# Moving the second layer's six matmuls in between the two parts of the attention result

## The chip, the cores and the metric

The kernel runs on one core of one Trainium2 chip. The time is the device time of one execution in microseconds. The median of four runs is compared; the profile is of one execution.

## The reference

Two stages follow each other, in float32. The first is a linear attention with a decaying state (batch 4, heads 8, sequence 768, head dimension 48):

```python
for t in range(S):
    cur = np.einsum('bhd,bhe->bhde', u[None] * kt, vt)
    y[:, :, t] = np.einsum('bhd,bhde->bhe', rt, state + cur)
    state = wt[:, :, :, None] * state + np.einsum('bhd,bhe->bhde', kt, vt)
```

Its output, turned to x of (B·S, H·D) = 3072 x 384, goes through a feed-forward layer with d_ff = 2048:

```python
h = x @ w_in
g = h - np.tanh(h)
return (g @ w_out).astype(np.float32)
```

## The kernel before, in words

**Blocks.** The 4 x 768 tokens are cut into eight blocks of 384 tokens (`NB`). The attention of a block is computed in chunks of 64 tokens (`L`), six to a block, for four pairs of heads; two heads of a pair lie on partitions 0 to 47 and 64 to 111. The attention of block 0 is computed ahead of everything by `boot`. Then the main loop (lines 626 to 666) runs over i = 0 to 7: it computes the feed-forward layer of block i (`here`, its input tile `xT`) and, in between, the attention of block i + 1 (`later`). So there are seven blocks in the loop that hold attention work; the last has none. "Block 0" below is the loop's turn i = 0.

**The feed-forward layer.** d_ff is cut into 16 chunks f of 128. For each f, `first` issues the first layer for 384 tokens: three float32 matmuls of 128x128 by 384, which the profile shows as six MATMULs into `hp` (line 471). It also issues six ScalarE operations, beginning with the copy of `hp` into `h` (line 478). The elementwise rest is five VectorE operations, issued in the next turn of f. `Second.add` issues the second layer: three float32 matmuls into three accumulators `acc` in PSUM, again six MATMULs in the profile (line 509). It runs three chunks late: at f the main loop adds chunk f − 3 (`LAG`), so at f = 13 it adds chunk 10. `hp` has one buffer in PSUM, `acc` three of one each, and the attention's `att` two.

**The attention's phases.** `plan` gives each f at most one phase of the next block's attention: level 1 and the levels 2 to 32 (the scores inside a chunk, by doublings), "turn" (transposes of the keys), "update" (the states at the six chunk borders, with VectorE operations at line 371), and "result" at f = 13. Each phase is issued between the first layer of its f and the second layer. The matmuls of a phase use 48- or 64-row pieces of the array.

**The result phase.** `result` adds up two products in two PSUM tiles `yp` (both buffers of `att`). Part one is 96 matmuls of the states with the decayed receptance `rp` (line 391). Then a drain of TensorE raises the semaphore `fence` (line 397) and TensorE waits for it (line 399). Part two is 96 matmuls of the values with the scores `A` onto the same sums (line 409). Four ScalarE copies take the result from PSUM into `late` and the three parts of the next block's `xT` (line 423). Then `fill_holes` issues six small DMAs on SP (line 431), which put the heads that lie in `late` into the 16-partition holes of `xT`. The next block's first layer at f = 0 reads `xT` with its holes.

**What sets the order.** The instructions of TensorE, SP, VectorE and ScalarE are issued in the order in which the code stands (`manual_schedule`). In one turn of f the order is: the first layer; the elementwise rest of f − 1; what `before` holds; the phase; what `behind` holds; the load of this f, if there is one (on SP, bound by `begin_behind` to start after the copy of `hp` of this f); the conversions of weights, in the turn i = 0 alone; the second layer of f − 3. At f = 13, `plan` has a load (of `wt`) only for i = 0; at f = 14 there is one of `kq` for i = 0 and of `rp` for the other turns.

Of the kernel before, what the change touches and what calls it, by code (L numbers as in the profile page):

```python
# [54 lines left out]
NPAIR = H // 2  # L55
# [29 lines left out]
def kernel(  # L85
# [79 lines left out]
    def convert(f, raw, _):  # L165

        lo, hi = raw[:, :, 0], raw[:, :, 1]
        a = w_sb[:, f, :].bitcast(I32)
        up = conv.tile([P, 2 * DM], I32, name="up", tag="up", bufs=3)
        nc.scalar.activation(out=a.bitcast(F32), in_=hi.bitcast(F32), func=AF.Prelu,  # L170
                             scale=HIGH_SCALE, alpha=NEGATIVE)
        nc.scalar.activation(out=up, in_=lo.bitcast(U32), func=AF.Copy, scale=2.0 ** -29)
        return [
            lambda: nc.vector.tensor_single_scalar(a, a, 3, op=ALU.logical_shift_left),
            lambda: nc.vector.tensor_tensor(out=a, in0=a, in1=up, op=ALU.add)]  # L175


    def scratch(ps):
        return ps.tile([P, 2, BANK], F32, name="att", tag="att")
# [3 lines left out]
    class Block:  # L183
# [189 lines left out]
                        in1=kvp[:, c % 2, n0:n0 + D], op0=ALU.mult, op1=ALU.add)  # L373
            return ins

        def result(self, ps, pairs, holes_full=False):


            St, rp = states[self.q], self.tiles["rp"]
            yp = [scratch(ps) for e in range(2)]  # L380
            slots = [pairs[n:n + 2] for n in range(0, len(pairs), 2)]
            for n, slot in enumerate(slots):
                for c in range(NCP):
                    for par in range(2):
                        for p in slot:
                            for h in range(2):
                                rows = slice(64 * h, 64 * h + D)
                                e0 = 64 * (h ^ (p % 2))
                                t0 = p * NB + (2 * c + par) * L
                                n0 = (n * NCP + c) * L  # L390
                                nc.tensor.matmul(yp[p % 2][e0:e0 + 64, par, n0:n0 + L],  # L391
                                                 lhsT=St[rows, p, 2 * c + par, :],
                                                 rhs=rp[rows, t0:t0 + L],
                                                 start=(n == 0 and c == 0), stop=False,
                                                 skip_group_check=True)

            nc.tensor.drain().then_inc(fence, 1)
            fences.append(None)
            nc.tensor.wait_ge(fence, len(fences))
            for n, slot in enumerate(slots):  # L400
                for p in slot:
                    for c in range(NCP):
                        for h in range(2):
                            for par in range(2):
                                toks = slice(64 * par, 64 * par + 64)
                                e0 = 64 * (h ^ (p % 2))
                                f0 = p * D2 + h * D
                                n0 = (n * NCP + c) * L
                                nc.tensor.matmul(yp[p % 2][e0:e0 + D, par, n0:n0 + L],  # L409
                                                 lhsT=self.v[toks, c, f0:f0 + D],  # L410
                                                 rhs=A[toks, h, p, c, :],
                                                 start=False,
                                                 stop=(n == len(slots) - 1 and c == NCP - 1),
                                                 skip_group_check=True)
            copies = []
            for n, slot in reversed(list(enumerate(slots))):
                for p in reversed(slot):
                    src = yp[p % 2][:, :, n * NCP * L:(n + 1) * NCP * L].rearrange(
                        "e a (c t) -> e c a t", t=L)
                    dst = self.xT[:, p, :] if p < KC else self.late  # L420
                    dst = dst.rearrange("e (c a t) -> e c a t", a=2, t=L)
                    for rows in (slice(0, D), slice(64, 64 + D)) if holes_full else (slice(0, P),):
                        copies.append(nc.scalar.copy(out=dst[rows], in_=src[rows]))  # L423
            return copies[0]

        def fill_holes(self, engines):

            for n in range(2 * KC):
# [2 lines left out]
                engines[n % len(engines)].dma_start(out=self.xT[64 * h + D:64 * h + 64, i, :],  # L431
                                                    in_=self.late[src:src + 16, :])


        def phase(self, ps, name):
            if name == "level 1":
                for p0 in HALVES:
                    self.level_1(ps, p0)()
            elif name == "turn":
                for p0 in HALVES:  # L440
                    self.turn(ps, p0)
            elif name == "update":
                for p0 in HALVES:
                    self.update(ps, p0)
            elif name == "result":
                self.result(ps, list(range(NPAIR)))
                self.fill_holes([nc.sync])
            else:
                self.level(ps, name, 0, NPAIR)
# [67 lines left out]

    def plan(i):

        names = ("level 1", 2, 4, 8, 16, 32, "turn", "update", "result")  # L520
        if i == 0:

            steps = (1, 2, 3, 4, 6, 8, 10, 11, 13)
            before, behind = {0: ("totals 1", "kq", "rp")}, {1: ("totals 2",)}
            converted = (1, 3, 3, 4, 5, 7, 10, 10, 12, 13)
            loads = {f: "weights" for f in (1, 2, 3, 4, 6, 7, 8, 9, 10)}
            loads.update({5: "v", 11: "rmix", 12: "kmix", 13: "wt", 14: "kq", 15: "rp"})
        else:
            steps = (4, 5, 6, 7, 8, 9, 10, 11, 13)
            before = {0: ("kmix",), 1: ("rmix",), 2: ("totals 1",), 3: ("totals 2", "kq"), 4: ("rp",)}  # L530
            behind, converted = {}, ()
            loads = {2: "v", 5: "rmix", 7: "kmix", 9: "wt", 11: "kq", 14: "rp"}
        return dict(zip(steps, names)), before, behind, converted, loads
# [5 lines left out]
    def more_weights(queue):  # L539
        raws.append(load_weights(more_weights.n, queue))  # L540
        more_weights.n += 1
        return raws[-1][-1]
# [3 lines left out]
    def begin_behind(ins, dma):  # L546


        tc.add_manual_dep(dma.ins, ins.ins.name, mybir.DependencyInfo(
            mybir.DependencyClass.Sync, mybir.DependencyReason.DATA))  # L550
# [73 lines left out]
    ps_a = ctx.enter_context(tc.tile_pool(name="ps_a", bufs=2, space=PSUM))  # L624
    waiting, rest, extra = [], [], []
    for i, blk in enumerate(blocks):
        here = xT
        later = blocks[i + 1] if i + 1 < len(blocks) else None
        after = blocks[i + 2] if i + 2 < len(blocks) else None
        if later:  # L630
            xT = later.begin()
        phases, before, behind, converted, loads = plan(i)
        second = Second(blk.b * S + blk.q * NB, ps_d)
        for f in range(NF):
            g, next_rest, made = first(here, f, ps_d)
            waiting.append((second, f, g))

            for n, op in enumerate(rest):
                op()
                if n >= 2 and extra:  # L640
                    extra.pop(0)()
            for op in extra:
                op()
            rest = next_rest
            if later:
                for name in before.get(f, ()):
                    later.prepare(name)
                if f in phases:
                    later.phase(ps_a, phases[f])
                for name in behind.get(f, ()):  # L650
                    later.prepare(name)
            name, ins = loads.get(f), None
            if name == "weights":
                ins = more_weights(nc.sync)
            elif name == "v":
                ins = later.load_v() if later else None
            elif name and after:
                ins = after.load(name, {"r": rT, "k": kT, "w": wT}[name[0]], 0, NPAIR)
            if ins:
                begin_behind(made, ins)  # L660
            extra = []
            for _ in range(converted.count(f)):
                extra += convert(*raws.pop(0))
            if len(waiting) > LAG:
                s, fs, gs = waiting.pop(0)
                s.add(fs, gs)
    for op in rest:
        op()
    for s, fs, gs in waiting:
# [48 lines left out]
```

## Time and profile before

| | |
|---|---|
| median of 4 runs | 673.24 us (671.71 to 674.21) |
| profiled execution | 674.21 us, its span 672.5 us |
| mean granted TensorE clock | 0.982 |
| TensorE matmul (PE) busy | 644.9 us, 96% |
| TensorE weight loads (PEld) busy | 414.2 us, 62% |
| VectorE (DVE) busy | 545.4 us, 81% |
| ScalarE (ACT) busy | 489.0 us, 73% |
| HBM traffic | 47.19 MB read, 4.72 MB written |

PE is the matmuls, PEld the weight loads; one sequencer issues both, and a load can run beside a matmul. SPq is a DMA queue's issue on SyncE. In the timelines of the profile each line is a run of like instructions: start and length in microseconds from the start of the span, engine, line of the kernel, operation, out<-in by the program's names, tile shape and count. What stands in brackets is the engine's idle time ahead of it, and what ended it: "issue" where the profile shows nothing that it waited for, "PEq" for TensorE's own sequencer. The length of a run of matmuls goes to the end of its last one, which overlaps the next run, so steps between runs are read from start to start.

### The profile page before, as it was taken

The page shows a single profiled execution, that of the slowest core. Times are in us where ns is not written, and L with a number is a line of the kernel's source. Part 1 is how long each engine was busy: PE and PEld are TensorE (multiplying, and loading weights), DVE is VectorE, ACT ScalarE, POOL GpSimd, SP SyncE. Part 2 cuts the span into 40 slices and gives each one's busy share as a digit, 9 for nine tenths or more (in the row PEclk, how much of TensorE's full clock was granted, in tenths as well). Part 3 has the DMA queues.
Part 4 walks back from the last instruction along what each step waited for, and adds up shares of the span by engine and source line. Part 5 has one row for each costly group of instructions (what it writes and reads, how often), then busy time and mean ns, then how long its engine had stood idle before and what let it go on. Part 6 is the DMA issues. An engine that isn't in the chain of part 4 may idle for free.

```text
span 672.5 us, 19961 instructions
## 1 busy us (share of the span) xinstructions
PE 644.9 (96%) x8480; PEld 414.2 (62%) x8480; DVE 545.4 (81%) x1101; ACT 489.0 (73%) x966; POOL 4.6 (1%) x19
## 2 busy tenths in 40 slices
PE   5867999999999999999999999999999999999998
PEld 4745656566665666656665666656666566655554
DVE  7769998799877997589975998769986899746664
ACT  4668699885867767785776858677577867768785
POOL 2000000000000000000000000000000000000000
PEclk9958899999999999999999999999999999999999
DMA  8645254422111313121312222113131200000000
GB/s 318 226 166 186 84 173 158 147 75 90 56 51 54 117 52 96 56 72 49 96 49 57 72 80 66 50 55 109 60 95 38 91 2 3 2 11 35 1 0 35
DMA packets 30840, 54.36 MB, mean 81 GB/s; under 512 B 2336, under 2 KB 28704, under 8 KB 30752
## 3 DMA queue, kind: packets, MB, share of 16 engines
q1 hardware_dynamic: 30336, 52.80, 24.2%
q8 instruction: 66, 1.08, 0.7%
q10 hardware_dynamic: 352, 0.25, 0.1%
q14 instruction: 22, 0.18, 0.1%
q0 software_dynamic: 64, 0.05, 0.0%
HBM read 47.19 MB, written 4.72 MB: 77 GB/s over the span
## 4 chain that ended last, share of the span: by engine, by line
PE 74%; DVE 9%; ACT 5%; issue 5%; PEld 4%; DMA 1%; PEldq 1%; SPq 0%; DVEq 0%
PE acc L509 32%; PE hp L471 29%; PE att L242 8%; DVE states L371 2%; PE att L409 2%; PEld att L391 2%; PEld hp L471 2%; PE att L342 2%; DVE w_sb L175 1%; PEld acc L509 1%; DVE rp L274 1%; PE att L319 1%; DVE hs L488 1%; DVE scores L302 1%; ACT qb L481 1%
## 5 line engine op out<-in xcount | busy, mean ns | idle before, releaser
L471 PE MATMUL hp<-xT,w_sb 128*128 128x384 f32 x768 | 273.1, 492 | 3.2 <-ACT xT L423 2.1
L509 PE MATMUL acc<-w_sb,gT 128*128 128x384 f32 x768 | 275.8, 496 | 0.0
L471 PEld LDWEIGHTS hp<-xT,w_sb 128*128 128x128 f32 x768 | 147.7, 193 | 107.1 <-issue 3.6
L509 PEld LDWEIGHTS acc<-w_sb,gT 128*128 128x128 f32 x768 | 141.3, 191 | 89.5 <-ACT o L514 2.3
L478 ACT ACTIVATE h<-hp 128x384 f32<-128x384 f32 x128 | 62.8, 491 | 143.9 <-PE hp L471 143.2
L493 DVE TENSOR_TENSOR th<-h,th 128x384 f32<-128x384 f32 x128 | 70.9, 554 | 47.3 <-ACT th L482 47.2
L488 DVE SCALAR_TENSOR_TENSOR hs<-h,s 128x384 f32<-128x384 f32 x128 | 71.0, 555 | 26.6 <-ACT s L479 26.6
L496 DVE COPY_PREDICATED gT<-big,th 128x384 f32<-128x384 int32 x128 | 76.2, 595 | 12.8 <-ACT h L478 0.5
L480 ACT ACTIVATE qa<-s,shift 128x384 f32<-128x384 f32 x128 | 78.8, 615 | 4.2
L488 DVE SCALAR_TENSOR_TENSOR gT<-qb,hs 128x384 f32<-128x384 f32 x128 | 71.3, 557 | 9.2
L483 ACT ACTIVATE big<-s,shift 128x384 f32<-128x384 f32 x128 | 76.8, 600 | 0.0
L481 ACT ACTIVATE qb<-s,shift 128x384 f32<-128x384 f32 x128 | 76.7, 599 | 0.0
L488 DVE SCALAR_TENSOR_TENSOR hs<-qa,hs 128x384 f32<-128x384 f32 x128 | 70.5, 551 | 0.0
L479 ACT ACTIVATE s<-h 128x384 f32<-128x384 f32 x128 | 67.0, 523 | 4.0
L242 PEld LDWEIGHTS att<-rp,kq 48*64 48x64 f32 x3072 | 53.9, 146 | 22.0 <-issue 14.5
L482 ACT ACTIVATE th<-h 128x384 f32<-128x384 f32 x128 | 64.9, 507 | 0.0
L242 PE MATMUL att<-rp,kq 48*64 48x32 f32 x3072 | 57.8, 230 | 5.7 <-DVE rp L274 3.5
L274 DVE TENSOR_TENSOR kq<-kq,tot 128x768 f32<-128x768 f32 (+1 forms) x45 | 38.6, 859 | 3.1 <-PE att L242 1.6
L371 DVE SCALAR_TENSOR_TENSOR states<-states,tot,att 128x48 f32<-128x48 f32 x176 | 31.5, 256 | 9.1 <-PE att L360 9.1
L274 DVE TENSOR_TENSOR rp<-rp,tot 128x768 f32<-128x768 f32 (+1 forms) x45 | 38.8, 862 | 0.0
L302 DVE COPY_PREDICATED scores<-mask_all,att 128x384 f32<-128x384 uint8 (+1 forms) x54 | 31.9, 655 | 0.0
L242 PE MATMUL att<-rmix,kmix 48*64 48x64 f32 x768 | 14.5, 232 | 6.9 <-ACT rmix L222 6.9
(54 smaller groups left out, 338.2 us busy)
## 6 DMA issues: line engine op xcount, KB each, us to landing
raw<-in_weights SPq DMA_DIRECT2D x16, 768.0 KB, 4.4
rmix<-in_rT SPq DMA_DIRECT2D x7, 768.0 KB, 4.5
kmix<-in_kT SPq DMA_DIRECT2D x7, 768.0 KB, 4.8
wt<-in_wT SPq DMA_DIRECT2D x7, 768.0 KB, 4.5
kq<-in_kT SPq DMA_DIRECT2D x7, 768.0 KB, 5.5
rp<-in_rT SPq DMA_DIRECT2D x7, 768.0 KB, 4.7
v_sb<-in_v SPq DMA_DIRECT2D x8, 576.0 KB, 4.2
out_y<-o SPq DMA_DIRECT2D x23, 192.0 KB, 1.9
```

The source lines that it names most:

```text
L242: nc.tensor.matmul(dst, lhsT=lhs[rows, t0:t0 + L], rhs=src, start=True, stop=True)
L274: ins = nc.vector.tensor_tensor(out=part, in0=part, in1=by, op=ALU.mult)
L471: nc.tensor.matmul(hp, lhsT=w_in_sb[:, f, kc, :], rhs=xT[:, kc, :], start=(kc == KC - 1), stop=(kc == 0))
L479: nc.scalar.activation(out=s, in_=h, func=AF.Square)
L480: nc.scalar.activation(out=qa, in_=s, func=AF.Square, bias=shift[:, 0:1])
L481: nc.scalar.activation(out=qb, in_=s, func=AF.Square, bias=shift[:, 1:2])
L482: nc.scalar.activation(out=th, in_=h, func=AF.Tanh)
L483: nc.scalar.activation(out=big, in_=s, func=AF.Relu, bias=shift[:, 2:3])
L488: return lambda: nc.vector.scalar_tensor_tensor(out=out, in0=in0, scalar=scalar, in1=in1, op0=op0, op1=ALU.mult)
L493: lambda: nc.vector.tensor_tensor(out=th, in0=h, in1=th, op=ALU.subtract),
L496: lambda: nc.vector.copy_predicated(out=g, mask=big.bitcast(I32), data=th)], made
L509: nc.tensor.matmul(acc, lhsT=g[:, j * P:(j + 1) * P], rhs=w_out_sb[:, f, :], start=(f == 0), stop=(f == NF - 1))
```

## The change

The result phase is cut in two. `result_1` issues part one and the drain. `result_2` begins with the wait on `fence` and issues part two and the copies. In the main loop "result 1" stands where "result" stood, at f = 13; the second layer's six matmuls of that turn (chunk 10) come next; then "result 2" and the holes' DMAs. With them, the load and the conversions of that turn, which stood behind the result, now stand between its parts. `boot` calls both parts in a row as before.

```diff
-        def result(self, ps, pairs, holes_full=False):
+        def result_1(self, ps, pairs):
 ...
                                                  skip_group_check=True)
-
             nc.tensor.drain().then_inc(fence, 1)
             fences.append(None)
+            return yp, slots
+
+        def result_2(self, yp, slots, holes_full=False):
+
             nc.tensor.wait_ge(fence, len(fences))
             for n, slot in enumerate(slots):
 ...
+        def result(self, ps, pairs, holes_full=False):
+            return self.result_2(*self.result_1(ps, pairs), holes_full)
+
 ...
-            elif name == "result":
-                self.result(ps, list(range(NPAIR)))
+            elif name == "result 1":
+                self.parts = self.result_1(ps, list(range(NPAIR)))
+            elif name == "result 2":
+                self.result_2(*self.parts)
                 self.fill_holes([nc.sync])
 ...
-        names = ("level 1", 2, 4, 8, 16, 32, "turn", "update", "result")
+        names = ("level 1", 2, 4, 8, 16, 32, "turn", "update", "result 1")
 ...
             if len(waiting) > LAG:
                 s, fs, gs = waiting.pop(0)
                 s.add(fs, gs)
+            if later and phases.get(f) == "result 1":
+                later.phase(ps_a, "result 2")
```

## The prediction

> **What bounds the kernel now.** I read the page first: the shares, the fetch queue and the chain.
>
> ```profile
> span 672.5 us, 19961 instructions
> PE 644.9 (96%) x8480; PEld 414.2 (62%) x8480; DVE 545.4 (81%) x1101; ACT 489.0 (73%) x966; POOL 4.6 (1%) x19
> q8 instruction: 66, 1.08, 0.7%
> PE 74%; DVE 9%; ACT 5%; issue 5%; PEld 4%; DMA 1%; PEldq 1%; SPq 0%; DVEq 0%
> ```
>
> TensorE (PE) is busy 96% of the span and holds 74% of the chain, so a microsecond of its stream is a microsecond of the kernel. Queue q8 brings 66 packets, 1.08 MB, 16 KB each. The trace holds 17,096 TensorE instructions (8,480 weight loads, 8,480 matmuls, 136 of the sequencer): about 259 for each packet, so q8 is the fetch of TensorE's own program.
>
> Next the timeline of TensorE around an ordinary result phase (start, length, count):
>
> ```profile
> 190.81 2.10 PE L509 MATMUL acc<-w_sb,gT 128*128 128x384 f32 x6
> 192.74 2.10 PE L471 MATMUL hp<-xT,w_sb 128*128 128x384 f32 x6
> 194.77 1.63 PE L391 MATMUL att<-rp,states 48*64 48x64 f32 x96
> 196.51 1.56 PE L409 MATMUL att<-scores,v_sb 64*48 64x64 f32 x96
> 197.99 2.20 PE L509 MATMUL acc<-w_sb,gT 128*128 128x384 f32 x6
> 200.03 2.10 PE L471 MATMUL hp<-xT,w_sb 128*128 128x384 f32 x6
> 201.97 2.10 PE L509 MATMUL acc<-w_sb,gT 128*128 128x384 f32 x6
> ```
>
> The line at 192.74 is the first layer of chunk 13 (F13). L391 is part 1 of the result (R1), L409 part 2 (R2), the L509 at 197.99 the second layer's six matmuls (A10), 200.03 is F14, 201.97 A11. Where a six follows a six, the step is 1.93 or 1.94 us. Entering the small tiles it is 2.03 (192.74 to 194.77), and the first six after them takes 2.04: 0.10 for each side of a switch. R1 to R2 is 1.74.
>
> Then the weight loads of the phases at 117, 351 and 588 us:
>
> ```profile
> 117.05 1.30 PEld L409 LDWEIGHTS att<-scores,v_sb 64*48 64x48 f32 x87 [0.25 <-PEq L397]
> 119.48 0.22 PEld L409 LDWEIGHTS att<-scores,v_sb 64*48 64x48 f32 x9 [1.12 <-issue]
> 352.94 1.18 PEld L409 LDWEIGHTS att<-scores,v_sb 64*48 64x48 f32 x75 [0.25 <-PEq L397]
> 355.07 0.39 PEld L409 LDWEIGHTS att<-scores,v_sb 64*48 64x48 f32 x21 [0.95 <-issue]
> 591.11 0.29 PEld L409 LDWEIGHTS att<-scores,v_sb 64*48 64x48 f32 x15 [1.16 <-issue]
> ```
>
> In three of the seven phases of the main loop R2 breaks off and waits for nothing that the profile names. Counting the trace's TensorE instructions from one break to the next gives 6,400 and 6,401: 25 times 256. So the breaks sit at page ends of the program: the next 256 instructions are not there yet. R1 and R2 together issue 385 instructions in some 3.2 us, the only place in the loop where 256 are used up that fast. The program's packets lie where that needs them: starts at 117.18, 352.56 and 588.30, ends at 118.22, 353.48 and 589.63, and R2 resumes 1.26 to 1.59 us after each end.
>
> Last the copies and the small DMAs behind R2:
>
> ```profile
> 198.14 0.48 ACT L423 COPY late<-att 128x384 f32<-128x384 f32 x1
> 198.52 1.25 ACT L423 COPY xT<-att 128x384 f32<-128x384 f32 x3
> 199.80 3.68 SPq L431 DMA_DIRECT2D xT<-late  x6
> 203.58 0.52 SPq L196 DMA_DIRECT2D rp<-in_rT  x1
> ```
>
> **The change part by part.** Work is neither added nor removed: A10 and R2 change places in each of seven blocks. The drain stays at the end of R1; the start-up's two results keep their order.
>
> *The breaks.* A break costs the start of R2 to the start of A10 against the 1.49 us of the ordinary phase (196.50 to 197.99 in the weight loads). 117.05 to 119.77 is 2.72, a loss of 1.23; 352.94 to 355.55 is 2.61, 1.12; 588.71 to 591.48 is 2.77, 1.28. Sum 3.63 us. It reaches the end: R1 to R1 takes 78.21 and 78.22 us in blocks without a break (194.77, 272.98, 351.20) and 79.34 to 430.54, 1.12 more.
> Do they go? The page boundary 256 instructions before each break lies in R1, at pair 55, 43 and 49 of its 96; at 15.7 ns a pair that is 0.87, 0.68 and 0.78 us after R1's start, and R2 resumes 3.30, 3.19 and 3.36 us after it. That is what a page needs. With A10 between, R2 starts 1.74 + 2.14 = 3.88 us after R1 (next paragraph), and the page ends fall at its pairs 81, 69 and 75, at 14.8 ns each: needed at 5.08, 4.90 and 4.99 us, there at 4.17, 3.87 and 4.14. Margin 0.85 us or more. A boundary on R1's first instruction, the worst case, is needed 4.25 us later. So all three go: minus 3.63. Bounds: all gone, or all still there (0).
>
> *The switches.* Old, F13 to A11: 192.74 to 201.97, 9.23 us. New: F13 to R1 2.03; R1 to A10 1.74, as R1 to R2 (the drain's end releases it, and A10's first load, like R2's, can't start ahead); A10 to R2 2.14 (1.94, 0.10 as first six after small tiles, 0.10 for entering them); R2 to F14 1.48 (as 196.51 to 197.99); F14 to A11 2.04. Sum 9.43: plus 0.20 a phase, 1.4 us in seven. No row shows a six straight behind a drain: from 1.56, level 1's small tiles to their six (147.06 to 148.62), to 1.74 plus one exposed load of 0.19. I take 1.74, nearest to the row that has the drain. So 0.02 to 0.39 a phase, 0.1 to 2.7 in all.
>
> *The wait on the fence.* In the old order R2's first load starts 0.05 us behind the drain (0.24 idle in all). In the new one six matmuls, 2.14 us, lie in between, so the wait is over when reached; but the drain itself still holds A10. Saved: nothing, at most 0.05 a phase. If TensorE did wait there, F14 would be queued behind it.
>
> *What follows R2.* Copies, holes' DMAs and F14 all hang on R2. The next block's first six (F0) needs the last hole; its first load stands at 207.45, 9.39 after R2's end at 198.06. The last of six issues starts at 202.88 and lands 1.87 later, 204.75: 6.69 after R2. A10 no longer lies between, so F0 comes 7.46 after R2's end: slack falls from 2.7 to 0.77 us, about 0.7 with the event that TensorE spends on it (0.05). ScalarE runs its four copies, 1.7 us, within F14's 2.1, so they delay no h. SP: the six hole DMAs move behind nothing in later blocks, and rp's load (203.58) follows as before. In block 0 the load of wt, until now behind the holes (125.31), goes ahead of them. In that block two hole DMAs landed 4.0 and 3.5 us after issue, 8.3 after R2, with wt and kq just behind. Repeated, that stalls F0 by 0.9 us once; with wt gone ahead I take 0, and keep 0.9 for the range. Beyond 0.7 us, every further delay of the holes counts in full.
>
> *Sum.* 1.4 − 3.63 = −2.2 us. The profiled execution took 674.21 (span 672.5 and 1.7 around it): it becomes 672.0, its span 670.3. The median of the four runs is 0.97 lower: 673.24 − 2.2 = 671.0.
>
> **Two rules against it.** The Trainium skill, "Runtime: NRT & Kernel Launch", section "Instruction fetch mechanics", has the program come in blocks of 256 instructions and calls the cost of crossing one mostly hidden. The trace agrees on the 256 and not on the cover: 1.12 to 1.28 us in three places; by the page the sum would be plus 1.4. The skill's "TensorEngine Tiling (Array Packing)", section "Key Properties", lets every change of tiling mode drain the engine; the rows above price a side of such a switch at 0.10, and two more full drains a phase, at the 0.18 by which R1 to R2 exceeds level 1's step, would make 2.5 us of the 1.4, a sum of −1.1.
>
> **The rivals.** *The breaks stay* (TensorE fetches late for another reason, or the earlier wt load slows a page): only the switches are left, 673.24 + 1.4 = 674.6. For it: no row shows a page arriving unhurried in R2. Against: the 256 spacing, and the margin of 0.85. *The holes come late* (slower): F0 waits in each block. It decides from 0.7 us later behind R2 than today; a hole landing 4.0 instead of 1.9 us after issue, as in block 0, stalls 1.4 us, seven times 10: 671.0 + 10 = 681. Against: in the later blocks all land in 1.9. *The change does less than it says*: with drain and fence both kept, its nominal gain (the fence) is 0 to 0.35 us; alone, and at equal switches, that is 673.
>
> **How the numbers follow.** Forecast 75%, breaks stay 11%, holes late 7%, does less 7%. About 0.3%, 2.0 us, is what can be told from no change; the forecast sits just beyond it. With the switches at 0.1 to 2.7 it runs from −3.5 to −0.9, and to 0 with block 0's holes: 669.7 to 673.2; I give 0.50 of its 0.75 to faster by over 0.3% and 0.25 to within. Breaks staying: 0.09 within, 0.02 slower (with dearer switches). Holes late: 0.07 slower. Does less: 0.02, 0.02 and 0.03. Faster 0.52, same 0.36, slower 0.12. The range reaches to the rival at 674.6 less a little: 669.8 to 674.2.
>
> **What would show it.** Right: 96 unbroken L409 loads in all seven phases; F13 to A11 near 9.43; R1 to R1 near 78.4 everywhere; F0's load with no idle ahead. Wrong: an idle of 1 us by "issue" in L409 or A10; a wait of hp on the holes; a step R1 to A10 far from 1.74.

## The result, and the profile after

The changed kernel takes 671.04 us (median of 42 runs, 668.68 to 673.72), the kernel before 672.95 (median of 68): a ratio of 0.9971, 95% interval 0.9964 to 0.9978. That is 1.9 us less, 1.5 to 2.4 by the interval.

From the page of the changed kernel, the span, the busy time and the fetch queue:

```profile
span 668.4 us, 19960 instructions
PE 644.3 (96%) x8480; PEld 412.2 (62%) x8480; DVE 545.1 (82%) x1101; ACT 488.8 (73%) x966; POOL 4.6 (1%) x19
q8 instruction: 66, 1.08, 0.7%
```

The work is the same, and so are the 66 packets of TensorE's program. Its busy time hardly moved (644.9 to 644.3 us), so the difference lies in the time in which it stood idle.

The timeline of TensorE's matmuls around the result phase of block 1, now with L517 as the second layer, L479 as the first, and L412 as part two:

```profile
189.86 2.10 PE L479 MATMUL hp<-xT,w_sb 128*128 128x384 f32 x6
191.89 1.63 PE L391 MATMUL att<-rp,states 48*64 48x64 f32 x96
193.63 2.20 PE L517 MATMUL acc<-w_sb,gT 128*128 128x384 f32 x6
195.76 1.56 PE L412 MATMUL att<-scores,v_sb 64*48 64x64 f32 x96
197.25 2.20 PE L479 MATMUL hp<-xT,w_sb 128*128 128x384 f32 x6
199.28 2.10 PE L517 MATMUL acc<-w_sb,gT 128*128 128x384 f32 x6
```

From start to start the steps are 2.03, 1.74, 2.13, 1.49 and 2.03: 9.42 us, where the order before had 9.23. The new order is dearer by 0.19 in each block. What it buys is seen in the weight loads of the phases that had broken off. Blocks 0 and 3, with the six between the parts shown for block 0:

```profile
113.47 1.49 PEld L391 LDWEIGHTS att<-rp,states 48*64 48x64 f32 x96 [0.55 <-issue]
115.21 1.59 PEld L517 LDWEIGHTS acc<-w_sb,gT 128*128 128x128 f32 x6 [0.24 <-issue]
117.34 1.41 PEld L412 LDWEIGHTS att<-scores,v_sb 64*48 64x48 f32 x96 [0.55 <-issue]
348.71 1.49 PEld L391 LDWEIGHTS att<-rp,states 48*64 48x64 f32 x96 [0.55 <-issue]
352.58 1.41 PEld L412 LDWEIGHTS att<-scores,v_sb 64*48 64x48 f32 x96 [0.55 <-issue]
```

All 96 loads of part two stand in one run of 1.41 us, in all seven blocks. The 0.55 ahead of each part is the entry into the small tiles. Behind part two, here of block 1, come the holes' DMAs, and then the first load of the next block, with no idle time ahead of it:

```profile
199.05 3.68 SPq L434 DMA_DIRECT2D xT<-late  x6
204.77 1.80 PEld L479 LDWEIGHTS hp<-xT,w_sb 128*128 128x128 f32 x6
```

Part one to part one takes 78.41 or 78.42 us in every block; in the kernel before it was 78.21 or 78.22 without a break, and 79.45 and 79.33 behind the breaks of blocks 0 and 3.

From block 0's part one to the end of the span, the kernel before took 672.5 − 115.31 = 557.2 us and the changed kernel 668.4 − 113.47 = 554.9: 2.3 less. The rest of the difference of the two spans, 1.84, is the start-up, which the change doesn't touch. It differs as much between two executions of one kernel: 115.63 and 113.90 us to block 0's part one for the kernel split in blocks 0, 3 and 6, below. So spans of single executions are compared from there on, and the whole kernel by medians.

### The profile page after: what moved, and what is told of

Its sections match the earlier page's. It is cut to its first block, busy times and chain, and to the rows that moved or that the text cites. A ratio compares the mean times of both kernels' runs of the same rounds, so it can differ in the third digit from the quotient of the medians.

```text
span 668.4 us, 19960 instructions
## 1 busy us (share of the span) xinstructions
PE 644.3 (96%) x8480; PEld 412.2 (62%) x8480; DVE 545.1 (82%) x1101; ACT 488.8 (73%) x966; POOL 4.6 (1%) x19
## 3 DMA queue, kind: packets, MB, share of 16 engines
q8 instruction: 66, 1.08, 0.7%
## 4 chain that ended last, share of the span: by engine, by line
PE 92%; DVE 3%; DMA 2%; ACT 1%; issue 1%; PEld 0%; SPq 0%; PEldq 0%; DVEq 0%
PE acc L517 39%; PE hp L479 36%; PE att L242 9%; PE att L412 2%; PE att L342 2%; PE att L391 2%; PE att L360 2%; PE att L319 1%; DMA kq<-in_kT 1%; DMA raw<-in_weights 1%; DVE rp L274 1%; DVE tot L260 1%; DVE scores L249 0%; ACT scores L330 0%; DVE kq L274 0%
## 5 line engine op out<-in xcount | busy, mean ns | idle before, releaser
L479 PE MATMUL hp<-xT,w_sb 128*128 128x384 f32 x768 | 273.4, 493 | 3.3 <-ACT xT L426 2.1
L517 PE MATMUL acc<-w_sb,gT 128*128 128x384 f32 x768 | 275.2, 495 | 0.8
L479 PEld LDWEIGHTS hp<-xT,w_sb 128*128 128x128 f32 x768 | 146.4, 192 | 105.4 <-ACT h L486 2.4
L517 PEld LDWEIGHTS acc<-w_sb,gT 128*128 128x128 f32 x768 | 141.3, 191 | 90.6 <-issue 2.9
```

What stands on the lines that cost most here:

```text
L479: nc.tensor.matmul(hp, lhsT=w_in_sb[:, f, kc, :], rhs=xT[:, kc, :], start=(kc == KC - 1), stop=(kc == 0))
L517: nc.tensor.matmul(acc, lhsT=g[:, j * P:(j + 1) * P], rhs=w_out_sb[:, f, :], start=(f == 0), stop=(f == NF - 1))
```

## The experiments

In what follows a page is one packet of TensorE's program, 256 instructions, a page end is the place between two of them, and a pair is a weight load with its matmul. "Before" stands for the kernel before.

The theory: in part two TensorE waits for the next 256 instructions of its own program, which happens only where a page end falls into part one with part two straight behind it. The split gives the page 2.1 us more and costs 0.2 us of switches in every block. Rivals: the breaks belong to what blocks 0, 3 and 6 do (a load, a wait); or the six matmuls help in every block alike, by covering the fence or by the order of what follows.

**Moving the pages.** A few matmuls of the start-up are issued twice, so that everything behind them lies later in the program, by 196 or by 60 instructions.

```diff
+            self.again = 0
...
-                            nc.tensor.matmul(dst, lhsT=lhs[rows, t0:t0 + L], rhs=src,
-                                             start=True, stop=True)
+                            for _ in range(2 if self.again > 0 else 1):
+                                nc.tensor.matmul(dst, lhsT=lhs[rows, t0:t0 + L], rhs=src,
+                                                 start=True, stop=True)
+                            self.again -= 1
...
     def boot(ps, blk, later):
+        blk.again = 49
```

With 49 matmuls more in the order before:

> The kernel before, with 49 matmuls of the start-up issued twice: 196 more TensorE instructions ahead of the main loop, nothing else. Page theory: a break of part two sits 256 instructions behind a page end in part one, so the breaks move with the program's position. The first page end behind the start of part one lies 112, 6, 191, 88, 17, 170 and 99 instructions in, for blocks 0 to 6; with 196 more it lies 172, 66, 251, 148, 77, 230 and 159 in. Breaks are then in blocks 1 and 4 alone, after 64 or 65 and 70 pairs of part two, about 1.2 us each, and blocks 0, 3 and 6 are whole. Rival (something that these blocks do, a load or a wait, stops TensorE): blocks 0, 3 and 6 break as before. The time is of less use, since the start-up is longer by up to 1.5 us: 671.5 to 674.5.

Its weight loads of part two, now line 412, in blocks 1 and 4 (two runs each; in brackets the idle time between them):

```profile
195.18 0.96 PEld L412 LDWEIGHTS att<-scores,v_sb 64*48 64x48 f32 x64 [0.25 <-PEq L400]
197.14 0.52 PEld L412 LDWEIGHTS att<-scores,v_sb 64*48 64x48 f32 x32 [1.00 <-issue]
430.90 1.07 PEld L412 LDWEIGHTS att<-scores,v_sb 64*48 64x48 f32 x70 [0.24 <-PEq L400]
432.89 0.50 PEld L412 LDWEIGHTS att<-scores,v_sb 64*48 64x48 f32 x26 [0.93 <-issue]
```

The breaks are where the page ends put them, to the pair: after 64 in block 1 and 70 in block 4. Blocks 0, 3 and 6, which had broken before, run through. That rules out a cause in the blocks' own work. The period behind each break is 79.29 and 79.30 against 78.22, 1.07 to 1.08 us. From block 0's part one to the end it takes 670.9 − 115.22 = 555.7 us, 1.5 less than before, as one break less should give. The time, 672.65 against 672.51 for before in the same job, is one execution of each and tells nothing, since executions of one kernel lie up to 5 us apart.

With 15 matmuls more in the order before (`blk.again = 15`):

> The kernel before, with 15 matmuls of the start-up issued twice: 60 more TensorE instructions ahead of the main loop. Page theory: the page ends lie 52, 202, 131, 28, 213, 110 and 39 instructions behind the start of part one. Breaks of some 1.2 us in block 0 after 57 pairs of part two, block 5 after 86, block 6 after 51; in block 2 the page ends with part two, so the idle falls on the first weight load of the second layer behind it; block 3 (28) is open, since a page end 17 in gave no break before. So four or five breaks, and the loop 1 to 2.5 us longer than before. Rival: blocks 0, 3 and 6 break, at the old place.

Two full breaks came, after 57 pairs of part two in block 0 and after 86 in block 5. Here is block 0, and block 2, where the page ends with part two and the second layer (line 512) follows:

```profile
115.82 0.89 PEld L412 LDWEIGHTS att<-scores,v_sb 64*48 64x48 f32 x57 [0.25 <-PEq L400]
117.54 0.62 PEld L412 LDWEIGHTS att<-scores,v_sb 64*48 64x48 f32 x39 [0.83 <-issue]
274.68 0.19 PEld L512 LDWEIGHTS acc<-w_sb,gT 128*128 128x128 f32 x1
275.21 1.48 PEld L512 LDWEIGHTS acc<-w_sb,gT 128*128 128x128 f32 x5 [0.34 <-issue]
```

In block 2 the second layer's first load is followed by 0.34 us of idle, and the period is 78.64, 0.42 more than without a break. Between the two full breaks stand 10,752 TensorE instructions of the trace, 42 times 256. Block 6 (page end 39 instructions into part one) and block 3 (28) did not break, where four or five breaks were expected. The packets suggest why: block 6's page starts at 584.54, 1.2 us ahead of its part one (585.74), and block 3's at 348.08, 2.0 us ahead (350.10). So the page is asked for while the loads are still at least 39 instructions short of the page end, in the six before part one, and it has that much more time. A page end 52 instructions in (block 0) did break; where between 39 and 52 the limit lies, no run shows. From block 0's part one to the end it takes 670.0 − 114.08 = 555.9 us, 1.3 less than before, with two breaks and a small one instead of three; 1 to 2.5 more was expected.

The same 60 instructions ahead of the changed order:

> The changed kernel with the same 60 instructions more ahead of the main loop. Page theory: no break anywhere, since with six matmuls between the parts a page end 256 instructions behind any place of part one is needed 4.2 us or more later, and a page takes 3.4; part one to part one 78.4 us in every block, as in the changed kernel. If the changed kernel lost its breaks only because of where its pages happen to lie, breaks of about 1.2 us come back in some blocks.

No break in any block, and 78.41 or 78.42 us from part one to part one. So the changed kernel does not owe its unbroken runs to where its pages happen to lie, as far as this second place for them can show.

**Splitting some blocks only.** In four blocks, or in the other three, the second part follows the first at once.

```diff
                 if f in phases:
                     later.phase(ps_a, phases[f])
+                    if phases[f] == "result 1" and i % 3:
+                        later.phase(ps_a, "result 2")
...
-            if later and phases.get(f) == "result 1":
+            if later and phases.get(f) == "result 1" and i % 3 == 0:
```

The changed kernel beside them:

> The changed kernel once more, so that the next two are compared with it on one chip: 0.997 of before.

The split in blocks 0, 3 and 6:

> The parts are split only in blocks 0, 3 and 6, which had breaks; in blocks 1, 2, 4 and 5 they stand in a row as before. Page theory: the instruction count is the same, so no block breaks, and four of the seven switches at 0.20 us are saved: 3.63 - 0.6 = 3.0 us below before, 0.8 below the changed kernel, ratio 0.9955. Rival (the split gains the same in each block, by hiding the fence or the order of what follows): 3/7 of the gain, 1 us below before, 0.9986.

And the opposite, with the two conditions on `i` exchanged:

> The opposite: split only in blocks 1, 2, 4 and 5, in a row in 0, 3 and 6. Page theory: all three breaks stay and four blocks pay 0.20 us each: 0.8 us above before, ratio 1.0012. Rival (the same gain in each block): 4/7 of the gain, 1.1 us below before, 0.9983.

In this job the medians were 672.90 for before, 671.17 for the changed kernel (0.9982, 0.9967 to 0.9997), 670.52 for the split in 0, 3 and 6 (0.9967, 0.9952 to 0.9983) and 674.12 for the opposite (1.0024, 1.0013 to 1.0034). Both rivals with an equal gain in each block fall: splitting four blocks made the kernel slower. The two split kernels are 3.6 us apart; three breaks and one switch more are 3.8 by the prediction's prices. The timeline of weight loads of the split in 0, 3 and 6 shows both kinds of block, split (block 0) and in a row (block 1):

```profile
115.63 1.49 PEld L391 LDWEIGHTS att<-rp,states 48*64 48x64 f32 x96 [0.55 <-issue]
117.36 1.59 PEld L517 LDWEIGHTS acc<-w_sb,gT 128*128 128x128 f32 x6 [0.24 <-issue]
119.49 1.41 PEld L412 LDWEIGHTS att<-scores,v_sb 64*48 64x48 f32 x96 [0.55 <-issue]
194.04 1.49 PEld L391 LDWEIGHTS att<-rp,states 48*64 48x64 f32 x96 [0.55 <-issue]
195.78 1.41 PEld L412 LDWEIGHTS att<-scores,v_sb 64*48 64x48 f32 x96 [0.25 <-PEq L396]
```

No block breaks, and the period is 78.41 behind a split block and 78.22 behind one in a row. From block 0's part one to the end it takes 669.8 − 115.63 = 554.2 us, 3.0 less than before and 0.7 less than the changed kernel, as worked out. In the medians the intervals of these two kernels overlap. The opposite takes 672.6 − 114.23 = 558.4, 1.2 more than before; its three breaks have gaps of 1.10, 1.49 and 1.42 us between two loads where before had 1.24, 1.07 and 1.28, so the length of a break varies by some 0.4 from one profile to another. The longest, in block 3 of the opposite:

```profile
352.10 1.18 PEld L412 LDWEIGHTS att<-scores,v_sb 64*48 64x48 f32 x75 [0.24 <-PEq L396]
354.65 0.39 PEld L412 LDWEIGHTS att<-scores,v_sb 64*48 64x48 f32 x21 [1.37 <-issue]
```

The split in 0, 3 and 6 once more, in another job:

> The parts split in blocks 0, 3 and 6 alone, once more, so that the next one is compared with it on one chip. Page theory as before: 3.0 us below before, 0.9955; the first measurement gave 0.9967.

It took 669.75 us against 672.99 for before, 0.9962 (0.9949 to 0.9975).

**The drain.** It stands at the start of part two, behind the six, instead of the end of part one.

```diff
         def result_1(self, ps, pairs):
...
-            nc.tensor.drain().then_inc(fence, 1)
-            fences.append(None)
             return yp, slots
...
         def result_2(self, yp, slots, holes_full=False):
+            nc.tensor.drain().then_inc(fence, 1)
+            fences.append(None)
             nc.tensor.wait_ge(fence, len(fences))
```

> The changed kernel with the drain moved from the end of part one to the start of part two, behind the second layer's six matmuls. It tests the step of 1.74 us from part one to the six: if the drain is what makes it longer than the 1.56 of level 1, the step falls to 1.56 and the six's step to part two grows from 2.13 by the drain's 0.2, and the period stays at 78.4 us. If the drain costs nothing behind small tiles, the first stays at 1.74 and only the second grows.

Its weight loads in block 1:

```profile
191.82 1.49 PEld L391 LDWEIGHTS att<-rp,states 48*64 48x64 f32 x96 [0.55 <-issue]
193.38 1.59 PEld L517 LDWEIGHTS acc<-w_sb,gT 128*128 128x128 f32 x6
195.69 1.41 PEld L412 LDWEIGHTS att<-scores,v_sb 64*48 64x48 f32 x96 [0.72 <-PEq L400]
```

Part one to the six falls from 1.73 to 1.56, the six to part two grows from 2.13 to 2.31, and the period stays at 78.41 or 78.42. So the drain costs 0.17 to 0.18 us on either side of the six, and the split does not hide it.

**The whole result behind the six.** Part one and part two in a row, after the second layer.

```diff
-                if f in phases:
+                if f in phases and phases[f] != "result":
                     later.phase(ps_a, phases[f])
...
                 s.add(fs, gs)
+            if later and phases.get(f) == "result":
+                later.phase(ps_a, "result")
```

> The whole result, both parts in a row, behind the second layer's six matmuls instead of ahead of them. Page theory: part one starts 12 instructions later, so page ends lie 100, 250, 179, 76, 5, 158 and 87 in: breaks stay in blocks 0, 3 and 6, six pairs earlier (81, 69 and 75), and as the number of switches is that of before, the time is that of before, 673 us. Rival (moving the six matmuls late against the result is what helps, by the order of what follows): no breaks, or a gain of 1 us or more.

The breaks are in blocks 0, 3 and 6, after 81, 70 and 75 pairs; the one execution took 673.44 us against 672.51 for before in that job. The breaks are there with the six ahead of both parts, so it is not enough that the six move; they must stand between the parts. But block 0's break is far longer than any other:

```profile
117.39 1.24 PEld L409 LDWEIGHTS att<-scores,v_sb 64*48 64x48 f32 x81 [0.25 <-PEq L397]
121.41 0.29 PEld L409 LDWEIGHTS att<-scores,v_sb 64*48 64x48 f32 x15 [2.77 <-issue]
```

In this order block 0's load of `wt` is issued ahead of the whole result, at 115.10; in the changed kernel it stands between the parts, at 114.86. Its packets run from 116 to 119 us, and the page's packet starts at 119.01. With that load back behind the result:

```diff
-            name, ins = loads.get(f), None
+            name, ins = loads.get(f) if (i, f) != (0, 13) else None, None
...
                 later.phase(ps_a, "result")
+            if (i, f) == (0, 13):
+                begin_behind(made, after.load("wt", wT, 0, NPAIR))
```

> The whole result behind the second layer's six, as before, but block 0's load of wt back behind the result. With that load ahead, the break of block 0 was 2.9 us, against 0.7 and 0.8 in blocks 3 and 6; the page's packet started at 119.01, when the load's packets had passed (from 116 to 119). If the page waited behind the load, block 0 now breaks for 0.7 to 1.3 us after 81 pairs. If the size has another cause, it stays at 2.9.

```profile
117.30 1.24 PEld L409 LDWEIGHTS att<-scores,v_sb 64*48 64x48 f32 x81 [0.25 <-PEq L397]
119.45 0.29 PEld L409 LDWEIGHTS att<-scores,v_sb 64*48 64x48 f32 x15 [0.91 <-issue]
```

The page's packet now starts at 117.02, and the break is 0.91. So in this pair of runs the page that met the load waited behind it.

**Part two later still.** It stands behind the first layer of chunk 14.

```diff
             g, next_rest, made = first(here, f, ps_d)
+            if later and phases.get(f - 1) == "result 1":
+                later.phase(ps_a, "result 2")
...
-            if later and phases.get(f) == "result 1":
-                later.phase(ps_a, "result 2")
```

> Part two one six later still, behind the first layer of chunk 14, whose six ScalarE operations now stand ahead of the copies of the result. In the changed kernel the last hole lands 0.77 us ahead of the next block's first load. By the rival of the prediction (the holes come late) that slack is gone: part two ends 1.9 us later against the first layer that needs it, so TensorE waits at least 1.2 us in each of seven blocks, and up to 3.0 if the copies also wait for ScalarE's 3.3 us of chunk 14: 8 to 21 us longer than the changed kernel. If the slack is larger than the landing times say, 671.

It took 699.54 us, 28 more than the changed kernel and more than expected. From its timelines, ScalarE's last operation of chunk 14 and the copies, the holes' DMAs, and the next block's first six:

```profile
207.12 0.60 ACT L491 ACTIVATE big<-s,shift 128x384 f32<-128x384 f32 x1
207.63 0.46 ACT L426 COPY late<-att 128x384 f32<-128x384 f32 x1
209.24 3.68 SPq L434 DMA_DIRECT2D xT<-late  x6
214.34 3.84 PE L479 MATMUL hp<-xT,w_sb 128*128 128x384 f32 x6 [2.29 <-DMA xT<-late]
```

Part two starts at 204.50 and ends near 206.1, but its copies start at 207.63, behind ScalarE's own chunk. TensorE waits 2.29 us for the last hole, and its six then take 3.84 us instead of 2.10. The clock granted to TensorE is 0.50 in the 3.4 us from 214.70 on, and 1.00 before; the same fall follows this wait in five of the seven blocks. Part one to part one is 80.94 us in the two blocks where the clock stayed at 1.00, and 82.59 to 83.23 where it fell, against 78.41 in the changed kernel. So the price of the rival in which the holes come late is 2.5 us a block from the wait, which the expectation had, and up to 2.3 more from the clock, which it had not. The order of the change stands 0.77 us short of that.

**Both lessons together.** The 60 instructions of the start-up, and the split where the pages then end badly.

```diff
+        blk.again = 15
...
-                    if phases[f] == "result 1" and i % 3:
+                    if phases[f] == "result 1" and i not in (0, 2, 5):
...
-            if later and phases.get(f) == "result 1" and i % 3 == 0:
+            if later and phases.get(f) == "result 1" and i in (0, 2, 5):
```

> The 60 instructions more ahead of the loop, and the parts split where pages then end badly: blocks 0, 2 and 5. Loop: no break, part one of block 0 to the end 554.2 us as with the split in 0, 3 and 6. Start-up: a page end lies 91 instructions into its first part one, and TensorE waited there 2.2 and 3.0 us for a page in the profiles of the changed kernel and of before; the two kernels with 60 instructions more had no wait there and reached block 0's part one at 114.08 and 112.34 us, against 113.4 to 115.7 in the others. So about 1 us more: 4 us below before, ratio 0.994. Rival (the start-up is bound by its loads, and the wait only moves): the same as with the split in 0, 3 and 6, 0.9955 to 0.997.

It took 669.24 us, 0.9947 (0.9928 to 0.9966) of before, the lowest of the kernels measured several times; its interval overlaps that of the split in 0, 3 and 6, run in the same job (0.9962, 0.9949 to 0.9975). The loop is as expected, 668.2 − 114.06 = 554.1 us without a break. The gain in the start-up was not shown: its profile reaches block 0 at 114.06, the other's at 113.90. Its start-up does run through part one, but breaks off in the scores instead (line 322); the second line is of the split in 0, 3 and 6 without the 60:

```profile
28.93 0.18 PEld L322 LDWEIGHTS att<-rp,kq 48*32 48x32 f32 x3 [2.76 <-issue]
35.24 0.29 PEld L391 LDWEIGHTS att<-rp,states 48*64 48x64 f32 x3 [2.08 <-issue]
```

So in these profiles the wait moved, as the rival had it.

## Why the prediction was right

- *The breaks.* All three are gone, and they are page ends: moved by 196 and 60 instructions, they came to the pair where the count put them. Their price was worked out as 3.63 us. Splitting where they are, and nowhere else, gave 557.2 − 554.2 = 3.0 us in the profile, that is 3.6 with its three switches; by the medians of the two jobs it gained 2.4 and 3.2 us.
- *The switches.* 9.43 us were worked out for the five steps and 9.42 measured; 0.20 a block was worked out and 0.19 measured (78.41 against 78.22). The value taken for a six straight behind a drain, 1.74, is what the timeline shows (191.89 to 193.63), and the drain behind the six shows that it is the drain: 1.56 without it.
- *The skill's rule on switches.* The Trainium skill, "TensorEngine Tiling (Array Packing)", section "Key Properties", has a drain at every change of tiling mode. Priced like the drain instruction, at 0.18, two of them a block made the prediction's estimate of −1.1; the 0.19 a block that was measured leaves a side of a switch at the rows' 0.10.
- *The fence.* Nothing was counted for it, and moving the drain moved the cost without changing it.
- *The holes.* Worked out was a slack of 0.77 us. In the changed kernel's block 1 the last hole lands at 204.00 and the first load that needs it starts at 204.77. In block 0 the holes land at 125.62 and the load starts at 126.35: the 0.9 us kept for the range did not come.
- *The sum.* −2.2 us forecast, −2.3 from block 0's part one to the end of the profile, −1.9 (−2.4 to −1.5) in the medians. That the median of 671.04 meets the forecast of 671.0 so closely is partly luck: the kernel before came out 0.3 lower over 68 runs than over the four, and the gain 0.3 smaller. The gain, 0.29%, lies just inside the 0.3% that the prediction gave as what can be told from no change, though its interval is clear of zero. The span was forecast at 670.3 and was 668.4; the start-up accounts for the difference.
- *What was too simple.* A page was given a fixed 3.2 to 3.4 us. Counted the same way, the other breaks of part two in these runs give 2.8 to 3.6. Behind a load it takes longer: with the whole result behind the six, block 0's page end was passed 0.79 us into part one, at 116.45, and part two went on at 121.41, 5.0 us later. With such a page, which is 1.7 us later, the changed kernel's margin of 0.91 in block 0 would not have held by this sum. The page was not late there, and its packet, at 114.99, was ahead of the load's, which run from 116. That is an order of arrival within about a microsecond, not a reserve. The worst case named, a page end on part one's first instruction, was none in these runs: page ends 6, 17, 28 and 39 instructions in gave no break even with the parts in a row.
- *The skill's rule on fetching.* The Trainium skill, "Runtime: NRT & Kernel Launch", section "Instruction fetch mechanics", calls a block's cost mostly hidden. In the loop the profiles agree where the large matmuls stand between the parts, and not where part two follows part one at once, where 0.8 to 2.8 us of idle stood in the lines above. By the page the sum would have been plus 1.4; the median fell by 1.9.

## What to carry to other kernels

An idle stretch of an engine by "issue", in the middle of a run of small instructions, should be counted in instructions. If the distance to the next such stretch is a multiple of 256, as the 6,400 and 10,752 here, the engine probably waits for its program, and shifting the program by some instructions tests it. The cure here was slower work between two dense runs, not less work. The cure costs its switches wherever it is applied, so it belongs only where a page end falls badly; a shift of the program by a few instructions moves those places. An instruction page was seen to queue behind a bulk load (5.0 us instead of 3.1 until part two went on), so a load is better kept out of the microseconds in which a dense run passes a page end.

## What the runs showed of the hardware that was not expected

- TensorE's program is asked for at least 39 instructions ahead of the weight loads: the packet that belongs to a page end 39 instructions into part one started 1.2 us before part one began.
- A page's packet took 0.9 to 1.6 us itself, but waited until 119.01 behind a load of 768 KB in one order, and started at 117.02 without it: breaks of 2.77 and 0.91 us at the same place.
- After waits of 2.3 us for the holes, TensorE was granted a clock of 0.50 for 3.4 us in five blocks of seven, and in block 1 six matmuls took 3.84 us instead of 2.10. The other two blocks had the same waits and kept 1.00.
- The start-up scatters by up to 1.7 us between executions of one kernel (113.90 and 115.63 us to block 0's part one), a part of the 5 us between the shortest and the longest run of each kernel.
